# An attention kernel: VectorE's exponential by two quadratics, one ring of buffers, and an order made with a short look-ahead

## The chip, the cores and the metric

The kernel runs on one core of one Trainium2 chip. A core has TensorE (PE in the profile, with its weight loads as PEld), VectorE (DVE), ScalarE (ACT), GpSimd (POOL) and SyncE (SP), which issues nearly all transfers. The metric is the device time of one run in microseconds; a time here is the median of several runs.

## The reference

The input x has 2048 rows of 512. Four layers follow one another, A, B, A, B, each as x = x + layer(layernorm(x)). Layer A is ordinary attention with 32 heads of 16 columns; layer B is linear attention with a softmax feature map.

```python
def _A_ref(x, wqkv, wo):
    qkv = (x @ wqkv).reshape(B, S, 3, H, Dh).transpose(2, 0, 3, 1, 4)
    q, k, v = qkv[0], qkv[1], qkv[2]
    scores = einsum("bhqd,bhkd->bhqk", q, k) * (Dh ** -0.5)
    o = einsum("bhqk,bhkd->bhqd", softmax(scores), v)
    return o.transpose(0, 2, 1, 3).reshape(B, S, D) @ wo

def _B_ref(x, wqkv, w_phi, wo):
    ...                                  # q, k, v as above
    pq, pk = q @ w_phi, k @ w_phi        # per head
    phi_q = concatenate([softmax(pq), softmax(-pq)])
    phi_k = concatenate([softmax(pk), softmax(-pk)])
    o = (phi_q @ (phi_k^T @ v)) / (phi_q @ sum(phi_k) + 1e-6)
    return o.transpose(0, 2, 1, 3).reshape(B, S, D) @ wo
```

## The kernel before, in words

The change is in layer A. Its attention works on groups: a group G is four heads (of eight such sets) by one block of 512 queries, so that a layer has 32 groups. A group has 16 steps kt, one for every 128 keys, and a step has two halves of two heads each. For one half PE computes the scores of 128 keys by two heads by 512 queries into a double bank of PSUM, in eight matmuls (`score_cols`, L1277). ACT turns this tile of 128 x 1024 into exponentials in SBUF (`scores`, L1284), and PE multiplies both halves of a step by the values and adds them into the group's two sums (`pvs`, L1327). A layer has 32 x 16 x 2 = 1024 such score tiles. The scores' bank pool `psS` has two buffers.

Around this, in the same stretch of time, PE does side work in small units of eight matmuls (`mm_cols`, L724): the value, key and query projections of the later three sets of eight heads ("octets"), and the output projection, in two parts (`part`, `tail`). VectorE empties their PSUM pairs (`values_task`, `kq_task`, `out_task`), normalises finished groups (`norm_task`) and, in the first layer, prepares the weights of layer B (`prep_b`, `prep_rest`). There are two PSUM pairs besides the scores' banks, named `double` and `pm` in the profile; a group's two sums take one for the length of a group.

A few score tiles go another way: their scores are put into a free side pair, and VectorE computes the exponential from them (`power_task`, L1286 to L1317). It does so for two blocks of 512 columns apart, in two operations that read PSUM (L1295, L1298) and six in SBUF (L1304 to L1315) for each: it rounds the score to a whole power of two, shifts that into the exponent's bits and multiplies by a polynomial of degree four of the rest. Only one such tile is in work at a time, since its buffer `px` has one copy.

The order of all engines but SP within attention is written out while the program is built. A loop in `attention` (from L1504) keeps a clock of PE, of ACT and of VectorE from fixed costs in microseconds, such as 0.217 for a score tile or a unit, 0.864 for a step's product and 0.904 for an exponential, and picks PE's next piece by rules: a score tile as soon as its bank is free, then a side unit or a product if it fits before the next score tile is due. A table of numbers, `RULES`, sets by groups of two how much a product may be late, whether it may be split in two halves of 256 queries (`HALF`), and whether VectorE may take a tile (`eager`). VectorE's own work is ordered by `Plan`, which picks by rank among what is ready.

SBUF buffers come from pools: `pp` (6 x 4 KB) for exponentials and, outside attention, for other tiles of that size; `px` (1 x 4 KB); `xt` in `xp` (3 x 4 KB) for blocks of x, weights in preparation and the like; `xn` in `xp` (4 x 2 KB) for normalised rows and VectorE's intermediate tiles.

Layer B's work is ordered in a similar way (`feed`, written out, and `flow`, planned) and uses the same pools.

## Time and profile before

| | us |
|---|---|
| median of 3 runs (2482.95 to 2492.96) | 2484.48 |
| span of the profiled execution, first to last instruction | 2479.1 |
| first layer A's attention, first to last exponential | 70.96 to 1006.2 |
| second layer A's attention | 1306.1 to 2228.5 |
| exponentials on ACT, count | 1998 |

The profile is one execution on the chip. Its own time is given as the span; the median of the runs is 5.4 us longer. A row of a group gives the line, engine, operation, output and input by name, shapes and count, then busy time in us, the mean of one in ns, and the idle time just before, with who ended it. "issue" is time in which an engine waited for nothing that the profile shows. Matmuls are pipelined, so that a busy PE is not PE at its peak.

### The profile page before, as it was taken

Reading aid. Unit: us, or ns where it says so; the run is one execution under the profiler, and the core shown is the slowest. Engines: PE = TensorE matmul, PEld = TensorE weight load, DVE = VectorE, ACT = ScalarE, POOL = GpSimd, SP = SyncE. Lnnn points to the kernel's source line nnn. Section 1 sums busy time; section 2 is a strip of 40 time slices with the busy share of each in tenths; the row PEclk is TensorE's granted clock in tenths of the full one; section 3 lists DMA queues with packets and bytes.
Section 4 is the critical chain, followed back from the end, with each engine's and each line's share of the span. In section 5 each row is a group of like instructions: output and inputs, shape, how many; then the busy total and the mean of one; then the engine's idle time right before and its main releaser. Section 6 shows DMA issues by size and latency. Waiting matters only on the chain.

```text
span 2479.1 us, 110386 instructions
## 1 busy us (share of the span) xinstructions
PE 2307.3 (93%) x50122; PEld 1149.3 (46%) x50122; DVE 1640.5 (66%) x2914; ACT 2121.8 (86%) x2376; POOL 531.3 (21%) x644
## 2 busy tenths in 40 slices
PE   6999999999999999899899999999999999998998
PEld 4444554444444444445354444444444454444543
DVE  8466654555666546889973777667567562469897
ACT  6899999999999999544539999999999999993553
POOL 3111111121111000366441112112111000005553
PEclk9999999999999999999999999999999999999999
DMA  5410531142136421110123104203303421220003
GB/s 193 71 28 8 88 72 37 30 59 55 37 55 155 140 75 67 44 35 18 60 73 57 40 8 63 34 3 53 66 21 42 97 78 43 71 71 26 27 1 112
DMA packets 124025, 143.31 MB, mean 58 GB/s; under 512 B 65193, under 2 KB 70937, under 8 KB 122649
## 3 DMA queue, kind: packets, MB, share of 16 engines
q1 hardware_dynamic: 122360, 133.38, 22.2%
q8 instruction: 394, 6.46, 1.1%
q0 software_dynamic: 1184, 2.77, 0.3%
q14 instruction: 87, 0.70, 0.1%
HBM read 62.16 MB, written 41.94 MB: 42 GB/s over the span
## 4 chain that ended last, share of the span: by engine, by line
ACT 56%; PE 15%; DVE 13%; issue 12%; POOL 2%; SPq 1%; DMA 1%; POOLq 0%; ACTq 0%; DVEq 0%
ACT p L1284 55%; PE s L1277 3%; PE pm L1327 3%; PE double L1327 1%; PE pbv L1655 1%; DVE su L1728 1%; PE pk L1655 1%; DVE yt L1945 1%; PE pq L1655 1%; PE double L724 1%; DVE f L1720 1%; POOL f L1737 1%; DVE f L1721 1%; SPq L999 1%; DVE mx L1717 1%
## 5 line engine op out<-in xcount | busy, mean ns | idle before, releaser
L1284 ACT ACTIVATE p<-s 128x1024 f32<-128x1024 f32 x1998 | 1838.3, 1077 | 25.1 <-PE s L1277 23.6
L1277 PE MATMUL s<-kq 49*32 49x512 f16 x15104 | 793.4, 382 | 81.4 <-ACT p L1284 61.5
L1327 PE MATMUL pm<-p,v 64*32 64x512 f32 (+1 forms) x13216 | 805.5, 534 | 2.8 <-issue 2.8
L1277 PEld LDWEIGHTS <-kq 49*32 49x32 f16 x15872 | 388.8, 89 | 804.4 <-issue 704.8
L1327 PE MATMUL double<-p,v 64*32 64x512 f32 (+1 forms) x5848 | 320.6, 491 | 0.0
L1327 PEld LDWEIGHTS pm<-p,v 64*32 64x32 f32 x13216 | 262.2, 106 | 42.9 <-issue 7.3
L988 POOL TENSOR_TENSOR yt<-yt,yt 128x512 f32<-128x512 f32 x64 | 85.0, 1327 | 847.2 <-DVE yt L985 822.6
L985 DVE STREAM_TRANSPOSE yt<-pm 128x512 f32<-128x512 f32 x92 | 60.5, 695 | 207.4 <-PE pm L1327 207.4
L1655 PEld LDWEIGHTS <-xnTa 128*128 128x128 f16 x1152 | 111.0, 99 | 155.2 <-DVE f L1721 27.1
L1108 POOL TENSOR_TENSOR sq<-stg 128x512 bf16<-128x512 f16 x48 | 57.2, 1192 | 427.0 <-PE s L1277 266.3
L1737 POOL TENSOR_TENSOR f<-f,su 128x1024 f32<-128x1024 f32 x58 | 112.1, 1933 | 115.7 <-DVE su L1731 103.0
L1327 PEld LDWEIGHTS double<-p,v 64*32 64x32 f32 x5848 | 116.5, 106 | 21.1 <-issue 3.2
L1655 PE MATMUL pbv<-wbv,xnTa 128*128 128x512 f16 x384 | 92.8, 393 | 22.3 <-DVE f L1721 22.3
L1722 ACT ACTIVATE f<-f,c_pB 128x1024 f32<-128x1024 f32 x62 | 70.5, 1148 | 48.2 <-DVE f L1721 48.1
L1011 DVE TENSOR_SCALAR tq<-double,c_qk 128x512 f32<-128x512 f32 x36 | 26.8, 745 | 116.0 <-PE double L724 111.3
L724 PEld LDWEIGHTS <-wA 64*32 64x32 f16 x4608 | 75.5, 93 | 42.4 <-issue 3.6
L1361 DVE SCALAR_TENSOR_TENSOR xt<-pm,c_oA,xt 128x512 f32<-128x512 f32 x56 | 41.8, 746 | 80.5 <-PE pm L724 78.1
L1743 ACT ACTIVATE fk<-f 128x1024 f16<-128x1024 f32 x30 | 31.7, 1057 | 72.5 <-POOL f L1737 72.5
L985 DVE STREAM_TRANSPOSE vyt<-double 128x512 f32<-128x512 f32 x48 | 31.5, 692 | 87.9 <-PE double L724 84.7
L1655 PE MATMUL pq<-wbqk,xnTa 128*128 128x512 f16 x384 | 88.4, 379 | 0.8 <-DVE vt L1682 0.8
L1655 PE MATMUL pk<-wbqk,xnTa 128*128 128x512 f16 x384 | 88.1, 379 | 0.0
L1361 DVE SCALAR_TENSOR_TENSOR xt<-double,c_oA,xt 128x512 f32<-128x512 f32 x56 | 41.8, 746 | 68.2 <-PE double L724 67.6
(333 smaller groups left out, 3208.3 us busy)
## 6 DMA issues: line engine op xcount, KB each, us to landing
kq<-stg SPq DMA_DIRECT2D x168, 128.0 KB
xd<-xt SPq DMA_DIRECT2D x40, 512.0 KB
xt<-xd SPq DMA_DIRECT2D x40, 512.0 KB
v<-vyt SPq DMA_DIRECT2D x384, 16.0 KB
oD<-osp SPq DMA_DIRECT2D x24, 256.0 KB
ob<-oD SPq DMA_DIRECT2D x24, 256.0 KB
xt<-in_A_x_dram SPq DMA_DIRECT2D x8, 512.0 KB
wbqk<-dBqk SPq DMA_DIRECT2D x16, 256.0 KB
```

Source lines behind the costliest of these rows:

```text
L724: nc.tensor.matmul(ps[h][c, :], w[r, c], x[r], start=(n == 0), stop=(n == of - 1), skip_group_check=True)
L985: nc.vector.transpose(ys[u].rearrange("p a b -> p (a b)"), ps[u])
L988: nc.gpsimd.tensor_tensor(ys[0], ys[0], ys[1], ALU.add)
L1108: nc.gpsimd.tensor_tensor(sq, hi, hi, ALU.mult)
L1277: nc.tensor.matmul(banks2[u][32 * c:32 * c + 32, :], self.side(g, half, 64 * u, 0, kt * P + 32 * c, 32), self.side(g, half, 64 * u, 1, j * ...
L1284: nc.scalar.activation(pt, s, AF.Exp, scale=EXPS)
L1327: nc.tensor.matmul(acc[h][32 * hh:32 * hh + 32, part], self.oct[o]["v"][r, x:x + 32], pt[r, hh % 2, part], start=(kt == 0), stop=(kt == NT ...
L1361: nc.vector.scalar_tensor_tensor(xt[:, u, :], ps[h], con["oA"], xt[:, u, :], op0=ALU.mult, op1=ALU.add)
L1655: nc.tensor.matmul(dst, xnT[:, a, c, t * P:(t + 1) * P], w(b, c), start=(i == 0 and c == 0), stop=(i == 2 and c == NC4 - 1))
L1722: nc.scalar.activation(f, f, AF.Exp, scale=con["pB"])
L1737: nc.gpsimd.tensor_tensor(f3, f3, self.part_sums(f3, slice(0, 64), factor), ALU.mult)
L1743: nc.scalar.activation(fk[:, 0, :], ff, AF.Copy)
```

## The change

It has four parts.

**VectorE's exponential.** `power_task` is written anew. One operation turns the scores into whole numbers that are read as floating-point bits; one masks out the exponent, one the fraction; and two quadratics of the fraction, each in two operations, are multiplied in. All but the first work on 1024 columns at once, the first too when the scores lie in the pair `double`. The tile and two intermediate tiles are taken from the ring.

```diff
+            m = pp.tile([P, 2, 512], F32, tag="p", name="pm")
+            t = pp.tile([P, 2, 512], F32, tag="p", name="pz")
+            yi = pt.bitcast(I32)
...
+                nc.vector.tensor_scalar(yi, self.pair, 8192.0, FIELD * 2.0 ** 23, op0=ALU.mult, op1=ALU.add)
             self.freed(idx)
+            nc.vector.tensor_scalar(m.bitcast(I32), yi, KEEP, LEADM, op0=ALU.bitwise_and, op1=ALU.bitwise_or)
+            nc.vector.tensor_scalar(yi, yi, POWER, LEADE, op0=ALU.bitwise_and, op1=ALU.bitwise_or)
+            nc.vector.scalar_tensor_tensor(t, m, PA, m, op0=ALU.add, op1=ALU.mult)
+            nc.vector.scalar_tensor_tensor(pt, t, PB, pt, op0=ALU.add, op1=ALU.mult)
+            nc.vector.scalar_tensor_tensor(t, m, PC, m, op0=ALU.add, op1=ALU.mult)
+            nc.vector.scalar_tensor_tensor(pt, t, PD, pt, op0=ALU.add, op1=ALU.mult)
```

**One ring.** The pools `xp` and `px` are gone; all their tiles come from `pp` with 12 buffers of 4 KB, in pairs of rows for `xn`. The planner counts the free slots (`slots`); a side task asks for them before it takes one (`room`, `grab`) and gives them back at a planned time (`give`).

```diff
-    pp = pool("pp", bufs=6)
+    pp = pool("pp", bufs=RING4)
-    xp = pool("xp", bufs=3)
...
+        def room(self, n, keep=KEEP_SIDE):
+            return "until", lambda: sum(x <= self.plan.now for x in self.slots) >= n + keep
+        def grab(self, n=1):
+            for _ in range(n):
+                self.slots.remove(min(self.slots))
+        def give(self, wait=0.1, n=1):
+            self.slots += [max(self.plan.now, self.plan.end) + wait] * n
...
+                yield self.room(1)
+                self.grab()
+                xt = pp.tile([P, 2, D], F32, tag="p", name="xt")
...
+            if ln is None:
+                self.give(5.0)
```

**The order of attention.** `RULES` is gone. Before each piece PE gets, `look` tries all sequences of score tiles, products, half products, side units and waits for the next 2.6 us (`AHEAD_US`) and takes the first piece of the cheapest; a late exponential costs its lateness, waiting PE half of its time (`IDLE`), a split product 0.05. VectorE takes a tile whenever three ring slots and one more are free, a side pair is free and VectorE's clock is no more than 3.0 us ahead (0.4 before); several tiles may be in work at a time. The tile taken is 6 steps ahead, or 9 when another is in work (8 before).

```diff
-LEAD = 8
+LEAD = 6
+MORE = 9
+IDLE = 0.5
+PARTED = 0.05
+AHEAD_US = 2.6
-VBUSY = 0.4
+VBUSY = 3.0
...
+            def wants(pe):
+                if not tiles or sum(x <= pe for x in slots) < 3 + KEEP_POWER or plan.clock["V"] > pe + VBUSY or not pvq:
+                    return False
...
+                    if wants(pe) and min(self.pfree) <= pe:
+                        G, kt = aim()
+                        power.add((G, kt, 1))
+                        self.busy += 1
+                        self.grab(3)
```

**Keys and queries.** In `kq_task` the second clamp (L1019) goes, and POOL's square of the high part starts behind the low part (L1021), not behind the high part.

```diff
-            self.spawn(self.square_task(hi, sqs), self.plan.end - self.plan.now + 0.15)
-            yield "V", 0.43
-            nc.vector.tensor_scalar(tq, tq, CLAMP, -CLAMP, op0=ALU.min, op1=ALU.max)
             yield "V", 0.7
             nc.vector.tensor_tensor(lo, tq, hi, ALU.subtract)
+            self.spawn(self.square_task(hi, sqs), self.plan.end - self.plan.now + 0.15)
```

What this does to the order is seen on two engines. On ACT, before, the first layer's attention stands between the last square and value copy of the preparation (`sq`, `v`) and the first exponential of layer B (`f`):

```order
45 L1110 ACTIVATE sq<-stg 128x512 x2
46 L1103 ACTIVATE v_162<-pv__905 128x16x32
47 L1284 ACTIVATE p<-s 128x1024 x1002
48 L1722 ACTIVATE f<-f,c_pB 128x1024 x2
49 L1687 ACTIVATE vt<-pbv 128x32x16
```

The same place on ACT in the changed kernel:

```order
45 L1139 ACTIVATE sq<-stg 128x512 x2
46 L1132 ACTIVATE v_159<-pv__894 128x16x32
47 L1313 ACTIVATE p<-s 128x1024 x980
48 L1812 ACTIVATE f<-f,c_pB 128x1024 x2
49 L1777 ACTIVATE vt<-pbv 128x32x16
```

Of 1002 exponentials 22 have left ACT, and what stands on either side is unchanged; in the second layer the same row reads x996 before and x973 after.

On VectorE, before, a tile taken from ACT stands in a row of sixteen operations; this is the head of the first one, behind the end of a group (`yn`). `px` is the tile, `double` its scores, `pw` and `pz` are intermediate tiles:

```order
129 L1067 TENSOR_TENSOR yn<-yt_1875,rec 128x16x16
130 L1295 TENSOR_SCALAR px<-double 128x512
131 L1298 SCALAR_TENSOR_TENSOR pw<-px,double 128x512
132 L1295 TENSOR_SCALAR px<-double 128x512
133 L1298 SCALAR_TENSOR_TENSOR pw<-px,double 128x512
134 L1304 TENSOR_SCALAR px<-px 128x512
135 L1307 TENSOR_TENSOR pz<-pw 128x512
136 L1309 SCALAR_TENSOR_TENSOR px<-pz,px 128x512
137 L1311 SCALAR_TENSOR_TENSOR pz<-pw,pz 128x512
138 L1313 SCALAR_TENSOR_TENSOR px<-pz,px 128x512
139 L1315 SCALAR_TENSOR_TENSOR px<-pw,px 128x512
```

The last six operations come once more behind these, for the second half of the tile. The first such tile on VectorE in the changed kernel, with the end of a query block ahead of it (`stg`) and a group's sums behind it (`yt`):

```order
135 L1049 TENSOR_TENSOR stg<-tq,stg 128x512
136 L1328 TENSOR_SCALAR px<-double 128x1024
137 L1331 TENSOR_SCALAR pm<-px 128x1024
138 L1333 TENSOR_SCALAR px<-px 128x1024
139 L1335 SCALAR_TENSOR_TENSOR pz<-pm 128x1024
140 L1337 SCALAR_TENSOR_TENSOR px<-pz,px 128x1024
141 L1339 SCALAR_TENSOR_TENSOR pz<-pm 128x1024
142 L1341 SCALAR_TENSOR_TENSOR px<-pz,px 128x1024
143 L1016 STREAM_TRANSPOSE yt_2821<-pm_2091 128x512
```

A tile is now seven operations of 1024 columns instead of sixteen of 512 (eight where its scores lie in two separate banks, as for 33 of the 95). On PE, 349 products of a step are split in two halves of 256 queries, 214 before.

More of the change, by code (lines that the diff above doesn't have):

```diff
@@ L933, in take @@
                 return idx, psum_pair("pm")
[L934 to L935 removed]
+            self.pair = double()
+            return idx, [self.pair[:, h, :] for h in range(2)]
         def ring(self):
@@ L1389, in tail @@
             for t in (0, 2):
-                yield "until", lambda: ln.landed >= t + 2 and self.plan.clock["V"] <= self.plan.now + 0.2
+                yield "until", lambda: t in ln.xn and t + 1 in ln.xn and self.plan.clock["V"] <= self.plan.now + 0.2
                 yield "M", 4
```

365 lines of the change are left out of this document (209 added, 156 removed), and 3 rows, old and new, of the table RULES.

## The prediction

> **What bounds the kernel now.** I read the page first, then the windows of the five stretches, then who ended the waits on either side of the exponential.
>
> ```profile
> span 2479.1 us, 110386 instructions
> PE 2307.3 (93%) x50122; PEld 1149.3 (46%) x50122; DVE 1640.5 (66%) x2914; ACT 2121.8 (86%) x2376; POOL 531.3 (21%) x644
> ACT 56%; PE 15%; DVE 13%; issue 12%; POOL 2%; SPq 1%; DMA 1%; POOLq 0%; ACTq 0%; DVEq 0%
> L1284 ACT ACTIVATE p<-s 128x1024 f32<-128x1024 f32 x1998 | 1838.3, 1077 | 25.1 <-PE s L1277 23.6
> ```
>
> These are the page's busy times, the chain of waits by engine and the exponential's group. PE is busy longer than ACT, but matmuls overlap, so that figure says little; the chain gives ACT 56%, and the exponential alone is busy 1838.3 of 2479.1 us. The windows (start:end, then busy us of PE, PEld, DVE, ACT, POOL, then clock, DMA share, GB/s) place it:
>
> ```profile
> 0.00:70.96 70.96, 48.13 (x370) 32.43 (x370) 57.58 (x144) 40.14 (x60) 25.15 (x55) 0.95 0.58 192
> 70.96:1006.20 935.24, 891.46 (x22803) 437.61 (x22811) 540.44 (x1000) 922.23 (x1002) 113.05 (x107) 1.00 0.28 65
> 1006.20:1306.08 299.88, 265.59 (x1972) 136.51 (x1964) 265.59 (x444) 134.67 (x177) 156.60 (x254) 0.97 0.14 43
> 1306.08:2228.50 922.42, 878.29 (x23408) 434.45 (x23409) 556.78 (x979) 916.01 (x996) 111.21 (x103) 1.00 0.23 50
> 2228.50:2479.10 250.60, 223.82 (x1596) 108.30 (x1580) 220.13 (x348) 108.70 (x142) 125.27 (x125) 0.97 0.12 42
> ```
>
> The second and fourth rows are the two attentions, 1857.7 us together. There ACT is busy 922.23 of 935.24 and 916.01 of 922.42, so it idles 13.0 + 6.4 = 19.4 us, and it does nothing but 1002 and 996 exponentials: 0.920 us apiece in both. VectorE has 394.8 and 365.6 us free. So an attention lasts as long as its list of exponentials on ACT, and each one taken off that list is worth 0.920 us as long as PE brings scores in time. The other 621 us are bound elsewhere.
>
> ```profile
> PE s L1277 <- ACT p L1284: 63.9, 173, 0.5
> ACT p L1284 <- PE s L1277: 23.6, 31, 5.0
> ```
>
> In the waits (total, times, longest) PE waits for ACT 173 times and ACT for PE 31 times: PE is mostly ahead, with little to spare.
>
> **The exponentials on ACT.** The order has 980 and 973 on ACT instead of 1002 and 996, and 95 tiles on VectorE (44 and 51) instead of 50 (22 and 28). That is 45 x 0.920 = **-41.4 us** if ACT stays as full as now. The tile's scores are computed either way.
>
> **What one tile costs VectorE.** These are the groups that touch such a tile now, then the nearest rows for the new operations:
>
> ```profile
> L1295 DVE TENSOR_SCALAR px<-double 128x512 f32<-128x512 f32 x74 | 50.4, 681 | 9.8 <-PE double L1277 9.8
> L1298 DVE SCALAR_TENSOR_TENSOR pw<-px,double 128x512 f32<-128x512 f32 x74 | 50.5, 682 | 1.8
> L1304 DVE TENSOR_SCALAR px<-px 128x512 int32<-128x512 int32 x100 | 42.4, 424 | 0.0
> L1307 DVE TENSOR_TENSOR pz<-pw 128x512 f32<-128x512 f32 x100 | 68.2, 682 | 0.0
> L1309 DVE SCALAR_TENSOR_TENSOR px<-pz,px 128x512 f32<-128x512 f32 x100 | 70.3, 703 | 2.9
> L1311 DVE SCALAR_TENSOR_TENSOR pz<-pw,pz 128x512 f32<-128x512 f32 x100 | 72.5, 725 | 2.8
> L1313 DVE SCALAR_TENSOR_TENSOR px<-pz,px 128x512 f32<-128x512 f32 x100 | 71.8, 718 | 2.8
> L1315 DVE SCALAR_TENSOR_TENSOR px<-pw,px 128x512 f32<-128x512 f32 x100 | 72.6, 726 | 3.0
> L1728 DVE TENSOR_REDUCE su<-f 128x64 f32<-128x1024 f32 x60 | 72.7, 1212 | 9.1 <-ACT f L1722 8.2
> L1990 DVE SCALAR_TENSOR_TENSOR xt<-fl,c_oB,xt 128x1024 f32<-128x1024 f32 x13 | 16.3, 1260 | 5.1 <-PE fl L1987 5.1
> L567 DVE TENSOR_SCALAR lu<-lu 128x2 f32<-128x2 f32 x12 | 1.9, 161 | 0.0
> ```
>
> Before: 2 x (0.681 + 0.682 + 0.424 + 0.682 + 0.703 + 0.725 + 0.718 + 0.726) = 10.7 us, times 50 = 534 us. After, no row shows the three forms at full width. The read from PSUM: 1.26 (L1990, same width and source) to twice 0.681; I take 1.26, and 1.36 for the 33 tiles in two banks. A masking step: 0.424 (a full tile is no faster than half of one) to twice 0.424; a two-column step costs 0.161, so doubling the columns gives 0.424 + 0.263 = 0.69, which I take. A quadratic's half: 1.21 (L1728, one input from SBUF at this width) to twice 0.726; I take 1.25, beside L1990. One tile is 1.26 + 2 x 0.69 + 4 x 1.25 = 7.6 us (6.9 to 8.9), and 95 are 725 us: +191 us for VectorE.
>
> ```profile
> L1019 DVE TENSOR_SCALAR tq<-tq 128x512 f32<-128x512 f32 x48 | 20.9, 435 | 1.2
> L1021 DVE TENSOR_TENSOR stg<-tq,stg 128x512 f16<-128x512 f32 x48 | 54.1, 1128 | 0.9
> 485.10 1.19 POOL L1108 TENSOR_TENSOR sq<-stg 128x512 bf16<-128x512 f16 x1 [1.09 <-DVE rec L1062]
> 485.31 1.26 DVE L1067 TENSOR_TENSOR yn<-yt,rec 128x256 f32<-128x256 f32 x1
> 486.49 0.68 DVE L1021 TENSOR_TENSOR stg<-tq,stg 128x512 f16<-128x512 f32 x1
> ```
>
> The second clamp of a key or query block goes: -20.9 us. The low part took 1.128 on average but 0.68 in the last timeline row, clear of the square on POOL; with the square started behind it, 48 x 0.45 = -21 us. VectorE's net is +149 us, against 760 us free in the attentions: hidden on average, 75 us more in each of two stretches that have 365 free. Neither edit is on the path.
>
> The two middle rows show a two-input VectorE operation of 256 columns that holds until POOL's ends (486.57 against 486.29). [...]
>
> **PE.** The prices are differences of starts in the timeline:
>
> ```profile
> 479.97 0.41 PE L1277 MATMUL s<-kq 49*32 49x512 f16 x8
> 480.18 1.05 PE L1327 MATMUL pm<-p,v 64*32 64x512 f32 x16
> 481.04 0.41 PE L1277 MATMUL s<-kq 49*32 49x512 f16 x8
> ...
> 484.77 0.63 PE L1327 MATMUL pm<-p,v 64*32 64x256 f32 x16
> 485.20 0.41 PE L724 MATMUL double<-xnT,wA 64*32 64x512 f16 x8
> ```
>
> A score takes 0.21, a product with the values 0.86, half a product 0.43, so a split costs nothing beside the busy column's hint of 2 x 0.63 - 1.05 = 0.2. A side unit is eight matmuls of the score's length. An attention holds 1024 scores, 512 products and 612 units: 215 + 440 + 129 = 784 us, and some 25 us of transposes and folds by my estimate (24 groups of four to eight short matmuls, at about a product each). That is 809 us for 1002 exponentials, 0.81 each, and for 980, 0.83; ACT takes 0.920. PE's spare time falls from 0.11 to 0.09 us a tile: still positive, but it lies unevenly, so some scores come late. The look-ahead costs late starts directly and may split a product anywhere; it splits 349 instead of 214. I take these two against each other with +3 us: a few more late scores than the 31 now, at under a microsecond. Bounds: -19.4 (all idle gone) and +15 (the idle nearly doubles).
>
> **The ring.** The pools held 6 + 1 + 3 tiles of 4 KB and 4 of 2 KB, 48 KB; the ring holds 12 of 4 KB. New is that an exponential can get a slot whose last reader is a store:
>
> ```profile
> L1365 SPq DMA_DIRECT2D xd<-xt x28: 359/360/538, 747.5 to 2219.1; - x28
> DMA  0000000399999999995100400000000000000000
> 951.66 0.36 SPq L1365 DMA_DIRECT2D xd<-xt  x1
> ```
>
> The second row is one lone store of 512 KB in 40 slices of 0.125 us from 951.6: the engines are done after 19, at 2.4 us. The planner gives the slot back 5.0 us after the store, so the cover is 2.6 us; without it, each of 28 stores could hold ACT some 2.5 us, 70 us at the very most. SP issues loads of x into a ring slot now and waits for a product on PE instead of an older store; behind it on SP are the key and query loads of later groups. As a side task takes a slot only when the plan has it free already, I price both at 0. The stretches outside attention keep their order on ACT, so 0 with 2 us to either side.
>
> **Sum.** -41.4 + 3 = -38. The span would be 2441; the median lies 5.4 us above the profiled span, and I leave that distance alone: 2484.5 - 38 = **2446 us**.
>
> **The rivals.** *The idle goes too* (0.14): the look-ahead removes half or all of 19.4 us: 2424 to 2433. For it stands one unbroken run of exponentials (start, length, count at the end), so a full list is possible:
>
> ```profile
> 1323.31 457.11 ACT L1284 ACTIVATE p<-s 128x1024 f32<-128x1024 f32 x497 [0.33 <-PE s L1277]
> ```
>
> Against it, PE's spare time shrinks.
>
> *VectorE becomes the late engine* (0.13): its operations grow from 0.7 to 1.25 us and cannot be interrupted, so evacuations of side pairs and the tiles themselves come later and PE, in order, waits. It would need 20 us over 95 tiles, 0.2 us each: 2464. Against: after the change VectorE has about 285 us free in each attention.
>
> *PE runs out of instructions* (0.08, the slower side). The trace shows it once, where ACT starved:
>
> ```profile
> 796.00:810.00 14.00, 11.36 (x236) 6.24 (x230) 3.54 (x7) 9.33 (x10) 1.27 (x1) 0.88 0.95 314
> 1500.00:1600.00 100.00, 97.89 (x2615) 47.73 (x2600) 62.45 (x104) 99.78 (x110) 18.50 (x18) 1.00 0.32 45
> 802.77 0.63 PE L1327 MATMUL pm<-p,v 64*32 64x512 f32 x4 [2.55 <-issue]
> 804.63 1.02 ACT L1284 ACTIVATE p<-s 128x1024 f32<-128x1024 f32 x1 [3.89 <-PE s L1277]
> ```
>
> With the DMA engines 0.95 busy, PE waited 2.55 us for nothing the profile shows and ACT lost 3.89. 135 more splits are 135 x 32 more instructions, and a shorter span: 92431/1857.7 = 49.8 a us becomes 96750/1817 = 53.2. If a stall of 3.5 us came 16 times more, 56 us: 2484.5 - 41 + 56 = 2499; it decides from about 11 (break-even 41/3.9). Against it: the window from 1500 runs at 52.2 a us with ACT 99.78% busy. [...]
>
> *No net effect* (0.08): ring waits (28 x about 1.4 us) eat the gain, 2484.
>
> **How the numbers follow.** The forecast has 0.57, between 2436 and 2456. About 0.5% (12.4 us) is what a measurement of this kernel can tell from no change. Faster by more than that, under 2472: 0.57 + 0.14 + 0.13 = 0.84. Same 0.08, slower 0.08. The range leaves out the last two rivals and the lower end of the first: 2424 to 2472.
>
> **What would show it.** Right: 1953 exponentials on ACT near 0.920 us, idle in the two attention windows of 15 to 30 us, windows near 914 and 903 us, tiles of 7.6 us on VectorE with its busy time in each attention near 615 to 630. Wrong: ACT waiting for PE well over 40 us; PE waiting for px or for an evacuation on VectorE; "issue" waits on PE beyond 10 us; an exponential that waits for a DMA; a feed or flow stretch that moves by over 5 us.

## The result, and the profile after

The changed kernel takes 2568.53 us (median of 4 runs, 2561.77 to 2573.17), the kernel before 2483.72 us beside it (2480.23 to 2492.96): a ratio of 1.0343, 95% interval 1.0314 to 1.0372. It is slower by 85 us, where the forecast was faster by 38 us and the range ended at 2472.

From the page of the changed kernel, the lines that answer to those of before:

```profile
span 2560.0 us, 114673 instructions
PE 2329.1 (91%) x52282; PEld 1205.7 (47%) x52282; DVE 1795.6 (70%) x2764; ACT 2092.1 (82%) x2331; POOL 560.0 (22%) x644
ACT 32%; PE 26%; DVE 21%; issue 11%; SPq 5%; DMA 3%; POOL 2%; ACTq 0%; DVEq 0%; POOLq 0%
L1313 ACT ACTIVATE p<-s 128x1024 f32<-128x1024 f32 x1953 | 1809.2, 1068 | 132.0 <-PE s L1306 74.4
```

There are 1953 exponentials, as the order said, and they are busy 29 us less than before. But ACT's share of the chain falls from 56% to 32%, and the idle time before the exponentials rises from 25.1 to 132.0 us. In its place stand PE, VectorE and, new, SP's queue and the DMA engines. The windows of the same five stretches (start:end, length, then busy us of PE, PEld, DVE, ACT, POOL, then clock, DMA share, GB/s) say where:

```profile
0.00:73.05 73.05, 50.35 (x371) 33.47 (x371) 59.23 (x148) 39.98 (x60) 25.17 (x55) 0.91 0.55 187
73.05:1068.00 994.95, 899.98 (x24264) 466.17 (x24267) 623.43 (x944) 909.26 (x980) 126.97 (x107) 0.97 0.26 60
1068.00:1369.40 301.40, 272.04 (x1964) 138.11 (x1960) 264.87 (x441) 134.32 (x178) 156.65 (x254) 0.95 0.14 44
1369.40:2309.20 939.80, 882.12 (x24128) 460.04 (x24126) 629.58 (x888) 899.88 (x973) 125.97 (x103) 0.99 0.23 49
2309.20:2560.00 250.80, 224.62 (x1576) 107.91 (x1572) 218.47 (x345) 108.69 (x142) 125.23 (x125) 0.96 0.12 43
```

The three stretches outside attention are longer by 2.1, 1.5 and 0.2 us. The attentions are longer by 59.7 and 17.4 us. In them ACT is idle 994.95 - 909.26 = 85.7 us and 39.9 us, against 13.0 and 6.4 before. The whole difference of the two spans is 80.9 us = 106.2 us of idle, less 29.1 us of exponentials, plus 3.8 us elsewhere. So the question is where 106 us of idle come from. The waits in the first attention (total, times, longest):

```profile
PE s L1306 <- ACT p L1313: 62.4, 81, 15.1
ACT p L1313 <- PE s L1306: 47.6, 46, 11.8
ACT p L1313 <- DMA dAo<-ahlo: 21.6, 2, 15.3
PE double L745 <- DVE rec L1089: 11.4, 1, 11.4
ACT p L1313 <- DMA dF<-bf: 4.9, 1, 4.9
ACT p L1313 <- DMA xd<-xt: 3.7, 2, 2.8
```

Four of these lines have no like before. An exponential waits 30.2 us for stores: for a slot of the ring whose last reader is a transfer. And PE waits once for 11.4 us for VectorE, which is the longest wait of ACT for PE. Both lead to SP.

**A hole behind value blocks.** In the timeline, one row each of VectorE, PE and ACT (start, length, and in brackets the idle time before it and who ended it), then SP's queue:

```profile
122.35 1.31 DVE L1016 STREAM_TRANSPOSE vyt<-double 128x512 f32<-128x512 f32 x2 [11.99 <-DMA v<-vyt]
```
```profile
123.72 0.63 PE L745 MATMUL double<-xnT,wA 64*32 64x512 f16 x8 [11.37 <-DVE rec L1089]
```
```profile
124.89 1.02 ACT L1313 ACTIVATE p<-s 128x1024 f32<-128x1024 f32 x1 [11.78 <-PE s L1306]
```
```profile
110.64 39.58 SPq L1030 DMA_DIRECT2D v<-vyt  x55
```

VectorE has to empty the fourth pair of value sums into one of four buffers `yt`, which group sums use too. The one due is not free: it holds the first value block until that block's 16 transfers are out, and at 0.72 us each these end at 122.2 us. VectorE starts nothing else meanwhile; PE waits for the pair, and ACT for PE. SP had key and query loads and then weights to issue until 110.64 us, 37.6 us after attention began, and then needs 0.72 us for each transfer of 16 KB (the row ends at 55 of them with its window). The plan counted SP as free 15 us after the beginning. The same places in the trace of before, SP first (its row ends with its window too), then two rows of VectorE, the first of them the fourth value block:

```profile
109.02 31.17 SPq L999 DMA_DIRECT2D v<-vyt  x41
```
```profile
119.77 1.31 DVE L985 STREAM_TRANSPOSE vyt<-double 128x512 f32<-128x512 f32 x2 [2.09 <-PE double L724]
135.01 0.75 DVE L1011 TENSOR_SCALAR tq<-double,c_qk 128x512 f32<-128x512 f32 x1 [2.62 <-DMA v<-vyt]
```

And PE's last units for the fourth value block in the changed kernel:

```profile
108.96 0.84 PE L745 MATMUL double<-xnT,wAv 64*32 64x512 f16 x24
```

SP was as late before. But the old order gave VectorE the fourth block only at 119.77 us, when it waited for PE alone. The new order has it ready at 109.8 us, before SP has issued any transfer of the first block, and VectorE loses 11.99 us. Before, its longest wait for these transfers was 2.62 us.

**A hole behind a store.** VectorE's operations on the tile `ahlo` (count, shortest, median and longest in ns, first and last start), SP's queue, and ACT:

```profile
L412 DVE SCALAR_TENSOR_TENSOR ahlo<-awo,sAo_sc,ahlo x4: 745/752/1023, 497.2 to 525.2; 128x512 f16<-128x512 f32 x4
```
```profile
534.05 10.99 SPq L1030 DMA_DIRECT2D v<-vyt  x16
545.14 0.58 SPq L413 DMA_DIRECT2D dAo<-ahlo  x1
```
```profile
548.33 1.94 ACT L1313 ACTIVATE p<-s 128x1024 f32<-128x1024 f32 x2 [15.33 <-DMA dAo<-ahlo]
```

The tile is complete at 526 us, and the plan gives its slot back 8 us later. SP issues the store at 545.14, behind 16 transfers of a value block. The exponential that has this slot next starts at 548.33, after a wait of 15.33 us, and with it everything on ACT.

**What a hole costs besides.** Windows around the first hole, as above; the clock is the third figure from the end:

```profile
100.00:111.00 11.00, 10.34 (x290) 4.98 (x281) 2.63 (x4) 10.82 (x12) 1.84 (x2) 1.00 0.33 54
123.70:127.00 3.30, 3.29 (x64) 1.58 (x71) 1.58 (x3) 1.42 (x2) 1.27 (x1) 0.50 0.18 29
127.00:130.50 3.50, 3.50 (x76) 1.48 (x66) 0.00 (x0) 2.21 (x3) 0.00 (x0) 0.63 0.16 23
130.50:141.50 11.00, 11.00 (x344) 6.04 (x329) 3.59 (x5) 10.95 (x13) 1.48 (x1) 1.00 0.17 27
```

After the hole PE is busy throughout, but at a granted clock of 0.50 and 0.63, so that ACT gets scores for 3.63 us of work in 6.80 us: another 3 us. Ahead of the hole the clock was 1.00; it was 0.50 in the first 3.3 us behind PE's 11.4 us of idle, and 1.00 again from 6.8 us on. Behind the holes that end at 311, 513 and 548 us it was 0.50 too, in the 2.5, 2.6 and 3.7 us that follow (windows 311.5:314, 513.4:516 and 548.3:552).

### The profile page after: what moved, and what is told of

It is laid out like the page before. It is cut to its first block, busy times and chain, and to the rows that moved or that the text cites. A ratio compares the mean times of both kernels' runs of the same rounds, so it can differ in the third digit from the quotient of the medians.

```text
span 2560.0 us, 114673 instructions
## 1 busy us (share of the span) xinstructions
PE 2329.1 (91%) x52282; PEld 1205.7 (47%) x52282; DVE 1795.6 (70%) x2764; ACT 2092.1 (82%) x2331; POOL 560.0 (22%) x644
## 4 chain that ended last, share of the span: by engine, by line
ACT 32%; PE 26%; DVE 21%; issue 11%; SPq 5%; DMA 3%; POOL 2%; ACTq 0%; DVEq 0%; POOLq 0%
ACT p L1313 30%; PE pm L1355 7%; PE s L1306 6%; PE double L745 3%; SPq L1030 3%; PE double L1355 2%; PE pbv L1745 1%; PE pk L1745 1%; DVE su L1818 1%; DVE pz L1339 1%; DVE yt L2035 1%; DVE px L1341 1%; PE pq L1745 1%; DMA xd<-xt 1%; DVE yt L1016 1%
## 5 line engine op out<-in xcount | busy, mean ns | idle before, releaser
L1313 ACT ACTIVATE p<-s 128x1024 f32<-128x1024 f32 x1953 | 1809.2, 1068 | 132.0 <-PE s L1306 74.4
L1355 PE MATMUL pm<-p,v 64*32 64x256 f32 (+1 forms) x14160 | 802.4, 485 | 7.9 <-issue 7.9
L1306 PEld LDWEIGHTS <-kq 49*32 49x32 f16 x15872 | 378.8, 90 | 760.6 <-issue 645.5
L1355 PE MATMUL double<-p,v 64*32 64x512 f32 (+1 forms) x6632 | 378.7, 496 | 0.1
L1355 PEld LDWEIGHTS pm<-p,v 64*32 64x32 f32 x14160 | 296.2, 107 | 78.5 <-issue 22.6
L1019 POOL TENSOR_TENSOR yt<-yt,yt 128x512 f32<-128x512 f32 x64 | 94.7, 1480 | 913.4 <-DVE yt L1016 754.1
L1355 PEld LDWEIGHTS double<-p,v 64*32 64x32 f32 x6632 | 136.1, 107 | 26.3 <-issue 4.2
L1339 DVE SCALAR_TENSOR_TENSOR pz<-pm 128x1024 f32<-128x1024 f32 x95 | 121.6, 1279 | 1.5
L1341 DVE SCALAR_TENSOR_TENSOR px<-pz,px 128x1024 f32<-128x1024 f32 x95 | 119.6, 1259 | 1.4
L1337 DVE SCALAR_TENSOR_TENSOR px<-pz,px 128x1024 f32<-128x1024 f32 x95 | 119.4, 1257 | 1.2
L1335 DVE SCALAR_TENSOR_TENSOR pz<-pm 128x1024 f32<-128x1024 f32 x95 | 118.9, 1252 | 0.2
L1016 DVE STREAM_TRANSPOSE vyt<-double 128x512 f32<-128x512 f32 x36 | 23.8, 696 | 130.9 <-PE double L745 114.3
```

The costliest lines, as they stand in the source:

```text
L1016: nc.vector.transpose(ys[u].rearrange("p a b -> p (a b)"), ps[u])
L1019: nc.gpsimd.tensor_tensor(ys[0], ys[0], ys[1], ALU.add)
L1306: nc.tensor.matmul(banks2[u][32 * c:32 * c + 32, :], self.side(g, half, 64 * u, 0, kt * P + 32 * c, 32), self.side(g, half, 64 * u, 1, j * ...
L1313: nc.scalar.activation(pt, s, AF.Exp, scale=EXPS)
L1335: nc.vector.scalar_tensor_tensor(t, m, PA, m, op0=ALU.add, op1=ALU.mult)
L1337: nc.vector.scalar_tensor_tensor(pt, t, PB, pt, op0=ALU.add, op1=ALU.mult)
```

## The experiments

Each kernel was timed beside the kernel before in the same session, whose median was 2483.7 us beside the change and 2478.5 to 2482.9 us in the experiments. So kernels are compared below by the column "over before", a kernel's median less that of before in its own session. "Idle" is ACT's in the two attentions, window less ACT's busy time. The kernels with `short` or `few` in their names leave work out, so that they don't compute the reference's values.

| kernel | us | over before, us | ratio, 95% interval | on ACT | idle |
|---|---|---|---|---|---|
| before | 2483.72 | | | 1998 | 13.0 + 6.4 |
| the change | 2568.53 | 84.8 | 1.0314 to 1.0372 | 1953 | 85.7 + 39.9 |
| stores_pool | 2551.16 | 68.2 | 1.0244 to 1.0291 | 1953 | 71.2 + 46.1 |
| sp_clock | 2533.60 | 50.7 | 1.0194 to 1.0228 | 1959 | 55.4 + 21.1 |
| own_pool | 2520.19 | 37.3 | 1.0134 to 1.0168 | 1978 | 39.3 + 25.6 |
| short_tile | 2542.46 | 59.6 | 1.0231 to 1.0269 | 1953 | 75.9 + 28.0 |
| arith_only | 2483.20 | 2.9 | 0.9999 to 1.0022 | 1998 | 12.0 + 4.8 |
| own_pool_sp_clock | 2515.96 | 35.6 | 1.0112 to 1.0158 | 1981 | 35.3 + 23.9 |
| own_pool_sp_clock_short | 2500.91 | 20.6 | 1.0054 to 1.0098 | 1981 | 28.8 + 19.4 |
| own_pool_sp_clock_more | 2534.31 | 54.0 | 1.0199 to 1.0249 | 1960 | 45.6 + 45.4 |
| own_pool_sp_clock_stg | 2504.08 | 24.9 | 1.0061 to 1.0127 | 1981 | 34.0 + 11.3 |
| stores_pool_sp_clock_stg | 2503.75 | 24.6 | 1.0070 to 1.0135 | 1954 | 29.8 + 25.0 |
| half_width | 2544.57 | 65.4 | 1.0235 to 1.0295 | 1994 | 37.0 + 36.6 |
| few_transfers | 2528.46 | 48.6 | 1.0181 to 1.0215 | 1953 | 60.9 + 29.7 |
| few_transfers_short | 2504.08 | 24.2 | 1.0078 to 1.0111 | 1953 | 51.6 + 17.9 |
| values_two_queues | 2537.40 | 58.9 | 1.0215 to 1.0259 | 1953 | 66.2 + 33.3 |
| values_two_queues_plan | 2510.42 | 32.0 | 1.0100 to 1.0144 | 1959 | 41.4 + 33.3 |
| values_two_queues_own | 2501.57 | 23.1 | 1.0060 to 1.0107 | 1989 | 24.1 + 17.6 |

The theory is that SP's queue is late, and that the change ties VectorE (by the value blocks' buffers) and ACT (by the ring) to it. The rivals are that VectorE is late by its own work, that the look-ahead's order starves ACT, and that the new arithmetic is at fault.

### The arithmetic alone

The new arithmetic in the kernel before, in halves of 512 columns and in the order of before (`arith_only`):

```diff
-                nc.vector.tensor_scalar(y, ps[u], OFF, MAGIC, op0=ALU.add, op1=ALU.add)
+                nc.vector.tensor_scalar(yi[:, u], ps[u], 8192.0, FIELD * 2.0 ** 23, op0=ALU.mult, op1=ALU.add)
...
```

> The kernel before with one part of the change: the new arithmetic in VectorE's tile, in halves of 512 columns, so that it fits the old buffers; order of all engines, pools and the other parts as before, 1002 + 996 exponentials on ACT. A tile is 2 x (0.68 + 2 x 0.42 + 4 x 0.72) = 8.8 us instead of 10.7, 95 us less for VectorE. All theories: the arithmetic itself has no price, and since VectorE is hidden in the order of before, time 2474 to 2486 us, with idle on ACT of 12 to 20 us. Should the arithmetic be at fault, time over 2495 us.

It took 2483.20 us, 2.9 over before, no difference that can be measured. Its two attentions:

```profile
71.12:1005.16 934.04, 889.81 (x22800) 434.58 (x22808) 504.82 (x957) 922.00 (x1002) 113.57 (x107) 1.00 0.28 65
1306.49:2227.21 920.72, 878.49 (x23408) 435.43 (x23415) 509.27 (x924) 915.90 (x996) 111.33 (x103) 1.00 0.23 50
```

VectorE is busy 83 us less than before, and the attentions are 1.2 and 1.7 us shorter. In the old order VectorE's time is worth nearly nothing, and the arithmetic is not at fault.

### Four suspects, one at a time

The stores on POOL (`stores_pool`):

```diff
-            nc.sync.dma_start(dAo[:, :, 2 * i:2 * i + 2], hl)
+            nc.gpsimd.dma_start(dAo[:, :, 2 * i:2 * i + 2], hl)
...
```

> The changed kernel, with the stores out of ring buffers in attention (the folded weights, the split output weights, the rows of x) issued by POOL instead of SP; PE, ACT and VectorE keep their order instruction by instruction, with 980 + 973 exponentials on ACT. Ring theory (an exponential gets a slot whose last reader is a store that stands behind small transfers in SP's queue): the exponentials' waits for dAo, dF and xd in the first attention (21.6 + 4.9 + 3.7 us, and 5.2 us under issue) go, so that its window falls from 995 to 955 to 965 us, and the second attention (0.2 us of such waits) stays within 3 us: time 2528 to 2540 us. VectorE theory (longer operations and 45 more tiles make evacuations late): VectorE's work is unchanged, so the time is 2560 to 2573 us. Against both: if POOL's own work now stands behind a store that waits for VectorE, waits for sq, vyt or osp appear and the time is above 2573 us.

It took 2551.16 us, 17 less than the change and 11 above the range. Its first attention is 15.6 us shorter. Of the 30.2 us that exponentials waited for stores, 11.9 us are left (dAo 8.2, xd 2.0, dF 1.7). POOL's queue and ACT at the longest of them:

```profile
499.51 0.38 POOL L1071 PARTITION_ALL_REDUCE nma<-nmx  x1 [5.97 <-issue]
499.77 0.85 POOL L413 DMA_DIRECT2D dAo<-ahlo  x1
```
```profile
506.61 2.85 ACT L1313 ACTIVATE p<-s 128x1024 f32<-128x1024 f32 x3 [8.22 <-DMA dAo<-ahlo]
```

The tile is complete at 492.3 us here. Its store stands in a row on POOL too, behind a reduction that starts at 499.51, and is issued at 499.77. It then takes 6.8 us to land, the longer of the two stores of this kind that POOL issued:

```profile
DMA to landing us min/median/max: 5.2/6.0/6.8
```

SP's two, at 508.13 and 545.14 us with the change, had let go of their slots after 5.2 and 3.2. So of this wait a part is the queue's and a part the transfer's, and whether SP's key loads, under way at the same time, made it slow wasn't tested. The second attention, which had 0.2 us of such waits, is 7 us longer, though nothing but the stores of x was moved in it; why is not shown. So the waits are real and a shorter queue in front of a store takes most of them away, but another in-order queue is no cure.

SP's clock in the plan (`sp_clock`):

```diff
-            self.yts, self.sp = [0.0] * RING, 15.0
+            self.yts, self.sp = [0.0] * RING, 38.0
```

> The changed kernel with one number of the plan: SP is taken to be free for value blocks 38 us after attention begins instead of 15 (in the trace it reaches the first one 37.6 us after). The order is made anew: 986 + 973 exponentials on ACT, 89 tiles on VectorE. Queue theory (the look-ahead puts value blocks earlier, and SP cannot carry them off yet, so that a transposition on VectorE waits for a buffer with everything behind it): the 12 us hole at 125 us and the holes of 4.4 and 2.0 us early in the second attention go, 18 us, less 6 x 0.92 us for the exponentials that come back; the waits for stores remain at 20 to 35 us: time 2550 to 2562 us. VectorE theory: 6 tiles less, no more than 8 us gained from them in idle, taken back by 5.5 us of exponentials: 2563 to 2573 us.

It took 2533.60 us, 34 less than the change and well below the range. Its two attentions, and the last stretch:

```profile
73.20:1040.10 966.90, 894.15 (x24304) 465.36 (x24288) 583.31 (x909) 911.52 (x986) 127.85 (x107) 0.98 0.26 62
1341.96:2260.83 918.87, 868.38 (x24136) 450.98 (x24140) 605.52 (x837) 897.82 (x973) 131.57 (x103) 1.00 0.23 48
2260.83:2529.50 268.67, 232.37 (x1700) 113.00 (x1688) 236.20 (x398) 108.50 (x141) 125.26 (x125) 0.96 0.14 48
```

One number of the plan is worth 28 us in the first attention and 21 in the second, which is now shorter than before the change; but 18 us of that come back in the last stretch, where side work put off is still to be done. The early holes, 18 us, are gone; the rest of the gain came with the new order and isn't traced. Two new holes, of 11.9 and 7.2 us, stand near 600 us, the second behind a store of dAo again.

A pool of their own for loaded and stored tiles (`own_pool`):

```diff
-RING4 = 12
+RING4 = 9
-                xt = pp.tile([P, 2, D], F32, tag="p", name="xt")
+                xt = pp.tile([P, 2, D], F32, tag="xt", name="xt", bufs=3)
...
```

> The changed kernel with the ring undone for tiles that are loaded or stored: they have three buffers of 4 KB to themselves, as before the change, and the ring of exponentials, VectorE's tiles and normalised rows has nine. The look-ahead makes its order anew: 988 + 990 exponentials on ACT, 70 tiles on VectorE. Ring theory: no exponential waits for a store any more; idle on ACT falls from 126 to 50 to 85 us, and with 1978 x 0.92 us of exponentials and 625 us elsewhere the time is 2502 to 2538 us. VectorE theory: idle goes with VectorE's tiles, 126 x 70/95 = 93 us, and the time is about 2544 us. Look-ahead theory (the order itself starves ACT of scores): idle stays near 126 us, time 2570 to 2580 us.

It took 2520.19 us, within the range, with no exponential that waits for a store:

```profile
70.82:1025.14 954.32, 889.70 (x24016) 459.49 (x24016) 575.45 (x894) 915.03 (x988) 129.07 (x107) 0.99 0.27 64
1326.41:2266.21 939.80, 878.59 (x23360) 439.41 (x23353) 514.07 (x768) 914.21 (x990) 122.02 (x103) 0.99 0.23 49
```

The idle is halved, to 65 us. But nine slots hold fewer of VectorE's tiles, 70 instead of 95, and 25 exponentials go back to ACT, so that the second attention is as long as with the change. Since the waits for stores and VectorE's tiles both became fewer, this run alone doesn't part the two.

VectorE's tile made shorter, in the order of the change (`short_tile`):

```diff
-            nc.vector.scalar_tensor_tensor(t, m, PC, m, op0=ALU.add, op1=ALU.mult)
-            nc.vector.scalar_tensor_tensor(pt, t, PD, pt, op0=ALU.add, op1=ALU.mult)
```

> The changed kernel without the second quadratic of VectorE's exponential: two of seven full-width operations of each of 95 tiles are left out (so that their values are not exponentials), 95 x 2.52 = 239 us of VectorE's work; every other instruction keeps its place. VectorE theory: evacuations and tiles come in time again, ACT's idle falls from 126 us to 30 to 50 us, time 2485 to 2500 us. Ring and queue theory: only waits that VectorE ended last go (some 16 us of ACT for px, pz and rec, part of PE's for evacuations): time 2545 to 2563 us.

It took 2542.46 us: 25 less than the change, neither the 68 to 83 of the VectorE theory nor the 5 to 23 of its rival, but close to the latter. The large holes (12.1, 16.0, 6.2, 5.5 us) are all there; the idle in gaps under 1.5 us falls from 50 to 28 us (all idle of the two attentions, 125.6 and 103.8 us, less the gaps above that, 75.5 and 76.3 us). VectorE's own lateness is a second cause, and as far as these two steps show it the smaller one.

### The order of the change kept, SP's queue made shorter

Twelve of the 16 transfers of a block left out (`few_transfers`):

```diff
             for a in range(4):
-                for m in range(4):
+                for m in range(a, a + 1):
...
-            nc.gpsimd.memset(v[:, V8 - 16:V8], VONE)
+            nc.gpsimd.memset(v, VONE)
```

> The changed kernel with 4 of the 16 transfers that carry a value block out of vyt, one for each of four rows of squares; the other twelve are left out, and v is filled with a constant by POOL instead, so that the values are not the reference's. SP's queue is shorter by 24 x 12 x 0.72 = 207 us in the two attentions; the order on PE, ACT and VectorE, the ring and VectorE's work are those of the changed kernel. Queue theory: the holes that stood behind value blocks go or shrink to a third (11.8 us at 125, 4.9 at 311, 15.3 at 548, and 2.0 and 4.4 in the second attention: 38 us), those behind key and query loads stay (513, 795, 834): time 2522 to 2540 us. If SP's queue only hides VectorE's or PE's lateness, other waits take their place: 2555 us or more.

It took 2528.46 us, within the range: 36 less than the change.

```profile
72.38:1042.23 969.85, 897.45 (x24264) 464.76 (x24266) 622.88 (x942) 908.98 (x980) 131.03 (x105) 0.98 0.25 59
1343.68:2273.05 929.37, 878.45 (x24128) 456.21 (x24121) 632.93 (x889) 899.66 (x973) 129.41 (x102) 0.99 0.21 47
```

PE, VectorE and ACT have as much to do as with the change, in the same order, and the attentions are 25.1 and 10.4 us shorter. The 11.8 us hole has 4.2 left, the 15.3 us one 2.2; those of 4.9, 2.0 and 4.4 us are gone, and those behind key and query loads stay (6.6 and 5.4 us), each as expected.

With VectorE's tile short as well (`few_transfers_short`):

> The same, and the second quadratic of VectorE's tiles left out too (neither values nor these exponentials are the reference's): both suspects smaller at once, in the changed kernel's own order. If queue and VectorE's work add (38 + 26 us), time is 2496 to 2514 us and idle on ACT 50 to 65 us. If they are one cause seen twice, no more than 10 us below the kernel beside it.

It took 2504.08 us, 24 below its neighbour, where the short tile alone gave 25: the two causes add, and neither is the other seen twice. The idle, 69.4 us, stays above the 50 to 65 that were expected.

Leaving transfers out also spares the DMA engines (0.25 and 0.21 busy in the two attentions, 0.26 and 0.23 with the change). So the last step keeps all of them, and issues half from POOL, which has just written the block (`values_two_queues`):

```diff
-                    nc.sync.dma_start(dst[:, :, 33 * a + 1:33 * a + 33], yt[32 * a:32 * a + 32, m:16:4, :])
+                    (nc.gpsimd if m % 2 else nc.sync).dma_start(dst[:, :, 33 * a + 1:33 * a + 33], yt[32 * a:32 * a + 32, m:16:4, :])
```

> The changed kernel complete, with half of the 16 transfers of each value block issued by POOL, which has just written vyt and so waits for nobody there; order on PE, ACT and VectorE as in the changed kernel. SP's queue is shorter by 24 x 8 x 0.72 = 138 us. POOL issued the one store dAo in 0.85 us, so that 8 transfers cost POOL some 7 us a block, about what SP saves. Queue theory: two thirds of the 40 us that leaving out 12 of 16 gave: time 2538 to 2550 us. If POOL is slower at small transfers than SP, or its sums come late behind them, nothing is left: 2560 us or more.

It took 2537.40 us, 0.6 us below the range and 26 less than the change. How long each queue took to issue one of these transfers around the first hole (shortest, median, longest ns):

```profile
L1030 SPq DMA_DIRECT2D v<-vyt x17: 586/599/1186, 110.5 to 121.0; - x17
L1030 POOL DMA_DIRECT2D v<-vyt x11: 551/551/551, 105.2 to 121.8; - x11
```

The same bytes as with the change, and the DMA engines' share in the first attention is 0.26 in both: it is SP's time to issue that was short. Transfers of 16 KB held SP for 0.6 to 0.72 us apiece, and halving SP's share of them was worth 26 us with the DMA engines as busy as before.

### Remedies together

Own buffers and SP's clock (`own_pool_sp_clock`):

> The changed kernel with both edits: stored and loaded tiles in three buffers of their own, and SP's clock in the plan at 38 us. 994 + 987 exponentials on ACT, 67 tiles on VectorE. Queue theory (ring slots behind SP, and work on VectorE behind SP): the holes of 11.9 and 4.2 us that the kernel with its own pool still had early in the attentions go, idle falls from 65 to 40 to 50 us; with 1981 x 0.925 us and 625 us elsewhere the time is 2497 to 2510 us. Look-ahead theory (any order that it makes has its own holes): idle stays near 65 us, time about 2522 us.

It took 2515.96 us, between the two ranges. The holes of 11.9 and 4.2 us went, and a third place came up, at which the plan doesn't know of SP's queue. On VectorE:

```profile
578.23 0.43 DVE L1034 TENSOR_SCALAR stg<-tq 128x512 f16<-128x512 f32 x1 [11.35 <-DMA kq<-sh]
```

A key block is to be written into the staging tile `stg` from which SP still issues key and query loads. ACT loses 11.1 us at 582 us by it. With the short tile added (`own_pool_sp_clock_short`):

> The same, with the second quadratic left out of VectorE's 67 tiles (their values are then no exponentials): 67 x 2.52 = 169 us less of VectorE's work, the order unchanged. If what the queue leaves of the idle is VectorE's lateness, idle falls to 20 to 28 us, near the 19 us of the kernel before, and the time is 2475 to 2486 us. If it is the look-ahead's order itself, with too little margin on PE, idle stays at 40 to 50 us and the time within 6 us of the kernel beside it.

It took 2500.91 us with 48 us of idle: VectorE's work is worth 15 us here, and 11 us of idle, a part only. The idle is what the second theory gave, the time what neither did. The holes at the staging tile remain, 10.9 us in the first attention and 6.4 us in the second. With the plan told of that place (`own_pool_sp_clock_stg`):

```diff
             yield "n", STEPS * (o - 1) + 4
+            if o > 1:
+                yield "until", lambda: self.plan.now >= self.landed.get(2 * o - 1, FAR) - 6.0
             self.stage(o)
```

> The changed kernel with the own pool and SP's clock at 38 us, and a third place where the plan is told of SP's queue: the key and query projections of a later octet begin only when the loads that still read the staging tile have left SP by the plan's clock. 992 + 989 exponentials on ACT, as many in all as without it (1981). Queue theory: the hole of 11.1 us at 582 us, where VectorE waited 11.35 us to write stg, goes; idle falls from 59 to 45 to 50 us, time 2502 to 2508 us. Look-ahead theory: each new order has holes elsewhere, idle near 59 us, time 2513 to 2520 us.

It took 2504.08 us, with 45.3 us of idle, both within what the queue theory gave. The hole is gone, and the second attention has 11.3 us of idle. The three remedies that leave the ring at twelve (`stores_pool_sp_clock_stg`):

> The change's ring of twelve kept, with the three remedies that leave it whole: stores out of it on POOL, SP's clock at 38 us, and the wait for the staging tile in the plan. 982 + 972 exponentials on ACT, 94 tiles on VectorE. Queue theory: of the 76 us of idle that the kernel with SP's clock alone had, the staging hole of 12 us and 8 to 15 us of ring waits go: idle 45 to 55 us, 1954 x 0.928 + 50 + 628 = 2491, time 2486 to 2502 us, the best of the kernels with the ring, and level with the kernel before. If stores on POOL only trade one in-order queue for another, idle stays over 70 us, time 2515 us or more.

It took 2503.75 us, 2 us above the range. Its attentions are 936.5 and 923.9 us long, 2.7 us more together than before the change, with idle as forecast; but the last stretch is 266.6 us instead of 250.6, as with SP's clock alone. There ACT waits for VectorE, which has output projections left over:

```profile
2257.70 1.15 ACT L1814 ACTIVATE f<-f,c_pB 128x1024 f32<-128x1024 f32 x1 [20.62 <-DVE f L1813]
```

More tiles in the nine slots of the kernel with own buffers and SP's clock, without the wait for the staging tile (`own_pool_sp_clock_more`):

```diff
-KEEP_POWER = 1
+KEEP_POWER = 0
```

> The same two edits, and a tile for VectorE may start when three slots of the ring are free instead of four (KEEP_POWER 0): 983 + 977 exponentials on ACT, 88 tiles. If 21 tiles more cost no more than their share of lateness, idle is 50 to 60 us: 1960 x 0.925 + 55 + 625 = 2493, time 2488 to 2500 us. If nine slots are too few, exponentials wait for px or pz and idle is over 80 us: 2520 us or more.

It took 2534.31 us with 91 us of idle, 32 more than without the edit. The time is that of nine slots being too few, but the waits aren't: exponentials wait 24.0 us for slots of VectorE's tiles (px, pz) instead of 17.6, and 68.5 us for PE instead of 43.3. Why PE is later in this order isn't shown. VectorE's tile in halves of 512 columns, in the same kernel (`half_width`):

```diff
-            nc.vector.scalar_tensor_tensor(t, m, PA, m, op0=ALU.add, op1=ALU.mult)
+            for u in range(2):
+                nc.vector.scalar_tensor_tensor(t[:, u], m[:, u], PA, m[:, u], op0=ALU.add, op1=ALU.mult)
...
```

> The kernel with its own pool and SP's clock, with the last six operations of VectorE's tile done in two halves of 512 columns (0.42 and 0.72 us each instead of 0.69 and 1.26), so that an evacuation can come in between, at 1.2 us more of VectorE's time per tile. The plan gives 998 + 996 exponentials to ACT, 54 tiles to VectorE. If VectorE's lateness comes from the length of single operations, idle falls from 59 to 35 to 45 us: 1994 x 0.923 + 40 + 626 = 2506, time 2500 to 2512 us. If it comes from the amount of work, idle goes with the tiles' total time, 54 x 8.8 = 475 against 67 x 7.6 = 509 us, to 55 to 60 us, time 2520 to 2528 us.

It took 2544.57 us, above both ranges, with 73.6 us of idle. In the second attention ACT waits for ring slots that VectorE's longer tile holds:

```profile
ACT p L1300 <- DVE pz L1328: 16.9, 14, 4.1
```

Shorter operations don't help, in the order that the plan makes of them. Last, value blocks on two queues again, now with the plan told of it: first with the ring of twelve (`values_two_queues_plan`), then with everything else (`values_two_queues_own`):

> The same with the plan told of it: SP's clock at 38 us, 8 transfers a block in it, and the wait for the staging tile; ring of twelve, stores on SP. 984 + 975 exponentials on ACT. Queue theory: idle on ACT 45 to 60 us, time 1959 x 0.926 + 52 + 630 = 2496, 2486 to 2508 us. If POOL's transfers land late, VectorE waits for v<-vyt again: 2520 us or more.

> All remedies at once: own buffers for stored and loaded tiles, value blocks on two queues, SP's clock and the staging wait in the plan. 995 + 994 exponentials on ACT, 59 tiles on VectorE. Queue theory: idle no more than the 45 us of the kernel without the second queue; 1989 x 0.923 + 38 + 626 = 2500, time 2492 to 2506 us: with so many exponentials on ACT it can't beat the kernel before.

They took 2510.42 us, just above the range with 75 us of idle instead of 45 to 60, and 2501.57 us, within it. No version beat the kernel before: the best complete one, the last, is 23 us over it, with 9 exponentials fewer on ACT than before and 22 us more idle.

## Why the prediction was wrong, point by point

**The exponentials on ACT, -41.4 us: right in number, wrong in price.** 980 and 973, as read from the order. But each took 1809.1/1953 = 0.926 us instead of 0.920, so -29.1 us. One that starts after a gap doesn't overlap the one ahead: alone it took 1.02 us, two in a row 1.94 (the rows at 124.89 and 548.33), so that a gap costs 0.1 us. There are 100 gaps on ACT instead of 31, which makes 7 of the missing 12 us; the other 5 aren't traced.

**VectorE's tile, 7.6 us: right; hidden: wrong by some 25 us.** The groups of after, by form:

```profile
L1335 DVE SCALAR_TENSOR_TENSOR pz<-pm 128x1024 f32<-128x1024 f32 x95 | 118.9, 1252 | 0.2
L1339 DVE SCALAR_TENSOR_TENSOR pz<-pm 128x1024 f32<-128x1024 f32 x95 | 121.6, 1279 | 1.5
L1328 DVE TENSOR_SCALAR px<-double 128x1024 int32<-128x1024 f32 x62 | 75.5, 1218 | 14.7 <-PE double L1306 12.5 <-ACT p L1313 1.2 <-PE s L1306 0.8
L1333 DVE TENSOR_SCALAR px<-px 128x1024 int32<-128x1024 int32 x95 | 68.8, 725 | 1.5
```

1.22 + 2 x 0.72 + 4 x 1.26 = 7.7 us, and VectorE is busy 623 and 630 us, within the 615 to 630 given. Two of the four quadratic steps left out gave 25 us in the order of the change and 24 us without most of the holes behind value blocks; 83 us less of VectorE's work in the old order gave nothing. A step's row in detail (shortest, median, longest ns):

```profile
L1335 DVE SCALAR_TENSOR_TENSOR pz<-pm x95: 1182/1218/2317, 143.5 to 2114.0; 128x1024 f32<-128x1024 f32 x95
```

The four steps have medians of 1.22 us and means of 1.25 to 1.28, some 16 us over 380 of them. In the first attention 8 of 176 took over 1.23 us, and each of these overlaps an operation on POOL; 13 others overlap one too and stayed under that. So the second rival, VectorE late by 20 us, held beside the main cause, not in its place. It was given 0.13 as a case by itself and no term of the sum.

**Late scores, +3 us, at most +15: wrong.** This bound came from PE's mean spare time. Exponentials waited 74.4 us for PE. Of that, PE's own waits for VectorE can explain up to 30.4 us, the long one at 123 us first; the clock of 0.50 and 0.63 behind that one adds some 3 us, and the rest isn't traced.

**The ring, 0: this is the step that failed.** It was priced from the 28 stores of x and a lone one of them, issued at once and done in 2.4 us, against a slot given back after 5.0. A store in the attention isn't issued at once: it is 19 us behind its tile's last operation at 526 us, for all that SP issues in order stands ahead of it. The sum's own sentence, that the key and query loads of later groups are behind a ring slot's load on SP, saw the coupling in the other direction only. Of the waits in the first attention, 30.2 us are exponentials waiting for stores, 26.5 of them for stores of weights (`dAo`, `dF`), which the price left out; with the stores on POOL the time fell by 17 us. And a side task that takes a slot only when the plan has it free is safe only if the plan's fixed 5 to 8 us hold; for the store at 545 us it was 22.

**The same blindness in the order, priced at nothing.** The sum took the look-ahead for a matter of PE's time. It also moves value blocks forward, and each has 16 transfers that hold SP 11 us. The trace of before showed SP reaching the first block 38 us into attention, and VectorE waiting 2.62 us for such transfers; the prediction uses neither row. Shortening SP's queue alone, with the order of the change, gave 36 us.

**The rivals.** "No net effect" had the ring's waits as its mechanism, and these came to 30.2 us against the 28 x 1.4 that it put. That this is near is luck: it counted the stores of x, which made 3.7 us of it, and the rest are three waits for stores of weights. The rival failed because holes behind value blocks and VectorE's lateness came on top. "PE runs out of instructions" did not come: no trace shows that a wait of PE under "issue" is one for instructions, and these stayed short. PE's longest row under "issue" in the first attention is 4.2 us in 7 waits, none over 1.2 us, and 3.8 us in the second. Of the signs named in advance, three came: ACT waiting for PE over 40 us, PE waiting for an evacuation, an exponential waiting for a DMA.

**What is shown and what stays open.** In the order of the change, SP's queue costs 36 us at least (the key and query loads were left as they are) and two steps of VectorE's tile 24 to 25; with both smaller, 69 us of idle remain, 50 more than before. Waits for stores are still in it (20.2 us in the first attention, for xd and dAo), and the granted clock there is 0.98, against 1.00 before the change; how the rest divides between these and the look-ahead's own choices isn't settled, since no run kept the old order with the new ring. The change in keys and queries was never run by itself.

## What to carry to other kernels

A plan that fills engines more tightly leans on every time that it doesn't model: before you price a new order by the engines' spare time, follow one issuing queue through the trace, with the time from a tile's last operation to the issue of its store, and put that into the plan. A ring shared by tiles of the bottleneck engine and tiles that a queue empties ties that engine to the queue; give stored tiles buffers of their own, or the queue less to issue. And small transfers, of 16 KB here, can cost the issuing engine's time before they cost bandwidth: with the DMA engines 0.26 busy, to halve their number on one queue was worth 26 us.

## What was not expected of the hardware

One transfer of 16 KB holds SP on average for 0.69 us (16 in 10.99 us) to 0.72 us (55 in 39.58). Where the two engines shared a block, SP's median was 0.60 us and POOL's 0.55: POOL was not the slower one at issuing these. For a store of `dAo`, 512 KB, it was: 0.85 us at 499.77 us in `stores_pool`, against SP's 0.57 and 0.58 in the change. An operation that masks 1024 columns of int32 took 0.72 us, 0.30 more than on 512 columns before (0.424), close to the estimate of 0.69; the step that reads PSUM at full width took 1.22 us against twice 0.68 for two halves.
